# Moving the start addresses of hh, hl, xc0 and set 1's first W1 tile within SBUF to 160 and 96 modulo 256 bytes

## The chip, the cores and the metric

The kernel runs on one core of a Trainium2 chip. The metric is the time of one execution on the device in microseconds (us); the median of several executions is compared. Engines are named as in the profile: PE is TensorE's matmuls and PEld its weight loads, DVE is VectorE, ACT ScalarE, POOL GpSimd, SP SyncE, which here issues DMAs.

## What is computed

A linear-attention scan over 768 steps for 4 batches and 8 heads, a gated two-matrix layer, and then a layer of eight experts whose gate is balanced by eight Sinkhorn rounds. There are 3072 tokens of 384 numbers, 8 experts and 1024 hidden numbers in each. The change touches the experts alone, the last loop below.

```python
def _moe2_ref(x, w_gate, w1, w2) -> np.ndarray:
    N, D = x.shape
    E = w_gate.shape[1]
    logits = x @ w_gate
    ...
    out = np.zeros((N, D), dtype=np.float32)
    for e in range(E):
        h = np.maximum(x @ w1[e], 0.0)
        ye = h @ w2[e]
        out += P[:, e:e + 1] * ye
    return out.astype(np.float32)
```

## The kernel before

All large products are made of numbers in two parts, high and low, each kept as float32r: a product is three matmuls, high by high, high by low, low by high.

The expert stage runs over `n` = 0 to 63, here called phases: 16 pairs of hidden blocks (`k`), and for each the four batches of tokens (`sb`). A phase computes the hidden block of its tokens by a fast matrix product that needs 15 products in place of 18 (the list `ORDER`). Each of the 15 products is six matmuls into `zp` with 256 columns: the moving operand is a token factor `xc`, the stationary one (the weights) a W1 factor `w1c` (`z_prod`, line 881). The factors lie in four groups of 4, 4, 4 and 3 products: tiles `xc0` to `xc3`, and for W1 `w1c{set}{group}` in three sets that take turns. Phase `n` uses two sets: 0 and 1 for k = 0, 3, 6 ..., then 2 and 0, then 1 and 2, so each pair holds for four phases.

VectorE and ScalarE add the products up in `ct`; `h_hi` (line 894) writes the rectified result's high part `hh` on ScalarE and `h_lo` the low part `hl` on VectorE. Both tiles have 8 buffers of 2 x 256 float32.

The second product uses the hidden block as weights: `y_fill` (line 1051) queues 24 units for the tokens of the phase before; a unit is three matmuls into `yp` with 384 columns, `hh` by `w2h`, `hh` by `w2l`, `hl` by `w2h`, where `hh` and `hl` are stationary and `w2h`, `w2l` moving. After each of the 15 products `phase` (line 935) issues as many units as a table written out by hand says:

```python
    YN = dict(zip(ORDER, (3, 2, 0, 3, 3, 0, 1, 1, 1, 1, 2, 2, 2, 1, 99)))
```

So TensorE's row in a phase is six zp, nine yp, six zp, six yp, twelve zp, nine yp, and so on: 90 zp and 72 yp, with 13 stretches of yp between stretches of zp. Where the text speaks of a switch, it means one such change from zp to yp and back. In the first two phases there are fewer yp. After the last phase the remaining yp come in one run.

All matmuls go through one helper, line 114 of the kernel. Tiles are laid out one behind the other in pools; `spaced` (line 623) puts an unused tile ahead of a tag's first tile (or behind it), by the table `GAPS` (line 621) in words of four bytes, which shifts all that follows in that pool. A tag's buffers are used in turn, so a tile's address repeats.

The start addresses in SBUF that follow from it, modulo 256 bytes (further offsets within the tiles are multiples of 512 bytes for W1 factors, hh and hl, 1024 for token factors and 1536 for w2h and w2l):

| operand of the expert stage | role | before | after |
|---|---|---|---|
| `xc0` (group 0) | moving, zp | 224 | 96 |
| `xc1`, `xc2`, `xc3` | moving, zp | 96 | 96 |
| `w1c10` (set 1, group 0) | stationary, zp | 32 | 160 |
| the other eleven `w1c` | stationary, zp | 160 | 160 |
| `hh`, `hl`, 8 buffers each | stationary, yp | 32 | 160 |
| `w2h`, `w2l`, 4 buffers each | moving, yp | 96 | 96 |

In the stage before, pa and pb (128 x 384, moving `xhl`, weights `w1h`, `w1l`, `w2h`, `w2l` of that layer) have both operands at 96.

Of the kernel before, what the change touches and what calls it, by code (L numbers as in the profile page):

```python
# [12 lines left out]
F32R = mybir.dt.float32r  # L13
# [48 lines left out]
def tile_rwkv_moe_sinkhorn_moe(  # L62
# [21 lines left out]
    P = 128  # L84
# [13 lines left out]
    T = 256  # L98
# [77 lines left out]
    pools = {}  # L176
# [415 lines left out]
    XP_ = plan(XC, XB)  # L592
# [25 lines left out]
        return sums, high, low  # L618

    w1raw, w2raw, w1c, w2c, xc, xd = {}, {}, {}, {}, {}, {}  # L620
    GAPS = {'w2h2': 16, 'w2l3+': 16, 'w1c00': 16, 'xc0': 16, 'w1c10': 16, 'xc1': 16, 'w1c01': 16, 'w1c13+': 16}

    def spaced(pool, shape, dtype, tag, name):
        n_ = GAPS.pop(tag, 0)
        if n_:
            pool.tile([P, n_], F32, name="gap_" + tag)
        t = pool.tile(shape, dtype, tag=tag, name=name)
        n_ = GAPS.pop(tag + "+", 0)
        if n_:
            pool.tile([P, n_], F32, name="gap_after_" + tag)  # L630
        return t
# [16 lines left out]
    def sp_w1(i, g, eng, tmp_=None):  # L648
        if i >= NW:
            return ()  # L650
        n_ = len(WP_[g][4])
        k = i % 3
        if tmp_ is None:
            tmp_ = pools["m2"].tile([P, 4, P], F32, tag="w1s", bufs=2, name="w1s")
        t = spaced(pools["m2" if k == 2 else "w"], [P, 2, n_, P], F32R, f"w1c{k}{g}", f"w1c{k}{g}")
        w1c[i, g] = t
        sums, high, low = factors(WP_, g, WB, w1raw[i], tmp_, t, eng)

        def end():
            low()  # L660
            if g == NGR - 1:
                w1raw.pop(i)
                ld_w1(i + 2)

        return sums, high, end

    def sp_w2(i):
        if i >= NW:
            return
        t = w2raw.pop(i)  # L670
        k = i % 4
        pool = pools["m" if k < 2 else "m2"]
        hi = spaced(pool, [P, 2, DM], F32R, f"w2h{k}", f"w2h{k}")
        lo = spaced(pool, [P, 2, DM], F32R, f"w2l{k}", f"w2l{k}")
        nc.scalar.activation(hi, t, AF.Copy)
        nc.vector.tensor_tensor(lo, t, hi.bitcast(F32), op=ALU.subtract)
        w2c[i] = (hi, lo)
        ld_w2(i + 2)

    def x_tile(n, g):  # L680
        t = pools["w" if g < 2 else "m"].tile([P, 2, len(XP_[g][4]), T], F32R, tag=f"xc{g}", name=f"xc{g}")
        xc[n, g] = t
        return t

# [35 lines left out]
    def ld_x(n, g):  # L720
        if n >= NB2 * NS:
            return
        t = x_tile(n, g)
        nc.sync.dma_start(t.bitcast(F32), xd[n % NS, g])
# [167 lines left out]
        return pools["m"].tile([P, 2, T], F32, tag="ct", bufs=CT, name="ct")  # L892

    def h_hi(n, i, b_, src):
        hh = pools["m2"].tile([P, 2, T], F32R, tag="hh", bufs=HB, name="hh")
        hl = pools["m2"].tile([P, 2, T], F32R, tag="hl", bufs=HB, name="hl")
        hb[n, i, b_] = (hh, hl, src)
        nc.scalar.activation(hh, src, AF.Relu)  # L898

# [35 lines left out]
    def phase(n):  # L935
# [71 lines left out]
        def s15():  # L1007
            prod("f", 15, True, True)
            sub(ct["10"], ct["10"], bk["f"])
            h_hi(n, 1, 0, ct["10"])  # L1010
            add(ct["12"], ct["12"], bk["f"])

        def s12():
            prod("h", 12, True, True)
            add(ct["00"], ct["00"], bk["h"])
            h_hi(n, 0, 0, ct["00"])
            h_lo(n, 1, 0)

        def s7():
            prod("e", 7, False, True)  # L1020
            add(ct["8"], ct["8"], bk["e"])
            h_hi(n, 1, 1, ct["8"])
            h_lo(n, 0, 0)
# [72 lines left out]
    CT, HB = 8, 8  # L1096
# [154 lines left out]
```

## Time and profile before

| | |
|---|---|
| median of 3 runs | 1935.41 us (1935.39 to 1937.25) |
| the profiled execution's own time | 1937.41 us |
| its span, first to last instruction | 1935.7 us |
| PE busy | 1908.3 us, 99% |
| DVE busy | 1384.3 us, 72% |
| ACT, POOL busy | 685.5 us, 646.8 us |
| expert stage | from 441.8 us on |

The page lists busy time by engine, the chain of work that ended last, and the groups of like instructions. Matmuls are pipelined: the next begins while the last still drains, so the duration of one (279 ns for a zp matmul) is longer than the distance to the next. Distances are read from the timeline, whose rows give the start of each stretch of like matmuls in us with two decimals.

### The profile page before, as it was taken

How to read it: one execution, taken by the hardware profiler on the slowest of the kernel's cores; microseconds unless marked ns; L12 is line 12 of the kernel's file. 1: busy time of each engine (PE TensorE's matmuls, PEld its weight loads, DVE VectorE, ACT ScalarE, POOL GpSimd, SP SyncE). 2: the span in 40 equal slices, each digit the busy share in tenths (PEclk: the TensorE clock that was granted, in tenths of full speed). 3: DMA queues.
4: the chain of work that ended last, by engine and by line, in shares of the span. 5: the costliest groups of instructions: out<-in, count | busy, mean ns of one | idle time of the engine just before them, and what ended most of it. 6: DMA issues, size and time to landing. Idle time of an engine off the chain costs nothing.

```text
span 1935.7 us, 38115 instructions
## 1 busy us (share of the span) xinstructions
PE 1908.3 (99%) x15499; PEld 1860.5 (96%) x15499; DVE 1384.3 (72%) x2409; ACT 685.5 (35%) x1322; POOL 646.8 (33%) x867
## 2 busy tenths in 40 slices
PE   6999999999999999999999999999999999999999
PEld 3799999999999999999999999999999999999999
DVE  7865787765887886676767676667677767667666
ACT  6733333344333333333333333333333333333322
POOL 6756666635331313122222222222323231312200
PEclk9999999999999999999999999999999999999999
DMA  9622444346655555555555555556455555555453
GB/s 371 231 93 83 139 133 138 104 148 238 234 178 191 191 191 192 180 200 182 197 189 190 187 194 187 189 174 207 172 196 185 193 192 190 189 180 187 171 201 120
DMA packets 90495, 353.76 MB, mean 183 GB/s; under 512 B 10385, under 2 KB 34257, under 8 KB 64593
## 3 DMA queue, kind: packets, MB, share of 16 engines
q1 hardware_dynamic: 90320, 351.34, 52.5%
q8 instruction: 122, 2.00, 0.4%
q14 instruction: 53, 0.43, 0.1%
HBM read 329.67 MB, written 20.45 MB: 181 GB/s over the span
## 4 chain that ended last, share of the span: by engine, by line
PE 95%; DVE 2%; DMA 1%; ACT 1%; SPq 0%; issue 0%; DVEq 0%; ACTq 0%
PE yp L114 41%; PE zp L114 34%; PE po L114 5%; PE pa L114 5%; PE pb L114 5%; PE w34ps L114 1%; PE yt L114 1%; PE sc L114 1%; PE trn L114 1%; DMA nat_kn<-in_kn_dram 1%; PE up L114 1%; DMA raw<-in_moe_w_dram 0%; PE pl L114 0%; DVE cvp L229 0%; DVE Sn L384 0%
## 5 line engine op out<-in xcount | busy, mean ns | idle before, releaser
L114 PE MATMUL zp<-xc,w1c 128*128 128x256 f32 x5760 | 805.3, 279 | 1.1 <-DVE ct L906 0.6
L114 PEld LDWEIGHTS zp<-xc,w1c 128*128 128x128 f32 x5760 | 780.3, 188 | 4.2 <-DVE ct L909 1.4
L114 PE MATMUL yp<-w2h,hl 128*128 128x384 f32 x1536 | 518.5, 338 | 0.6 <-DVE hl L903 0.6
L114 PE MATMUL yp<-w2l,hh 128*128 128x384 f32 x1536 | 517.3, 337 | 0.0
L114 PE MATMUL yp<-w2h,hh 128*128 128x384 f32 x1536 | 514.9, 335 | 0.0
L898 ACT ACTIVATE hh<-ct 128x512 fp32r<-128x512 f32 x384 | 236.8, 632 | 532.8 <-DVE ct L906 268.6
L906 DVE TENSOR_TENSOR ct<-ct,zp 128x512 f32<-128x512 f32 x576 | 380.0, 683 | 50.9 <-PE zp L114 45.8
L616 POOL TENSOR_TENSOR w1c<-w1s,w1c 128x512 fp32r<-128x512 f32 (+1 forms) x120 | 126.8, 1057 | 790.1 <-PE yp L114 484.0
L913 ACT ACTIVATE ct<-zp 128x512 f32<-128x512 f32 x256 | 153.5, 600 | 451.1 <-PE zp L114 451.1
L114 PEld LDWEIGHTS yp<-w2h,hl 128*128 128x128 f32 x1536 | 288.6, 188 | 1.0 <-DVE hl L903 0.9
L114 PEld LDWEIGHTS yp<-w2h,hh 128*128 128x128 f32 x1536 | 288.6, 188 | 0.2 <-issue 0.2
L114 PEld LDWEIGHTS yp<-w2l,hh 128*128 128x128 f32 x1536 | 288.6, 188 | 0.0
L1078 DVE SCALAR_TENSOR_TENSOR acc<-yp,Pm,acc 128x384 f32<-128x384 f32 x336 | 205.6, 612 | 108.2 <-PE yp L114 108.1
L903 DVE SCALAR_TENSOR_TENSOR hl<-ct,hh 128x512 fp32r<-128x512 f32 x384 | 274.8, 729 | 0.0
L909 DVE TENSOR_TENSOR ct<-ct,zp 128x512 f32<-128x512 f32 x128 | 88.0, 687 | 165.2 <-PE zp L114 165.2
L909 DVE TENSOR_TENSOR ct<-zp,ct 128x512 f32<-128x512 f32 x128 | 88.3, 690 | 76.0 <-ACT ct L913 40.7
L616 POOL TENSOR_TENSOR w1c<-w1raw,w1c 128x128 fp32r<-128x128 f32 (+1 forms) x90 | 55.9, 621 | 202.4 <-ACT w1c L612 202.4
L608 POOL TENSOR_TENSOR w1s<-w1raw 128x128 f32<-128x128 f32 x240 | 120.7, 524 | 0.2
L483 POOL TENSOR_TENSOR gl<-gs,gh 128x384 fp32r<-128x384 f32 x64 | 72.9, 1139 | 109.9 <-ACT gh L479 106.8
L114 PE MATMUL pa<-xhl,w1h 128*128 128x384 f32 x384 | 101.7, 345 | 1.3 <-ACT w34s L255 1.3
L114 PE MATMUL pb<-xhl,w2h 128*128 128x384 f32 x384 | 98.1, 336 | 0.4 <-DVE cv L230 0.4
L474 DVE TENSOR_TENSOR gs<-pb,asb 128x384 f32<-128x384 f32 x64 | 35.4, 552 | 68.3 <-PE pb L114 49.5
(130 smaller groups left out, 1908.9 us busy)
## 6 DMA issues: line engine op xcount, KB each, us to landing
xc<-xd SPq DMA_DIRECT2D x192, 1024.0 KB, 4.9
xc<-xd SPq DMA_DIRECT2D x64, 768.0 KB, 4.3
xd<-x2s SPq DMA_DIRECT2D x53, 256.0 KB, 2.7
w1raw<-in_e_w_dram SPq DMA_DIRECT2D x32, 384.0 KB, 3.1
w2raw<-in_e_w_dram SPq DMA_DIRECT2D x32, 384.0 KB, 3.1
raw<-in_moe_w_dram SPq DMA_DIRECT2D x8, 1024.0 KB, 9.3
nat_w<-in_w_dram SPq DMA_DIRECT2D x24, 264.5 KB, 3.6
nat_k<-in_kt_dram SPq DMA_DIRECT2D x24, 256.0 KB, 4.4
```

What stands on the lines that cost most here:

```text
L114: nc.tensor.matmul(o, lhsT, rhs, start=start, stop=stop, **kw)
L474: nc.vector.tensor_tensor(t, m_t.pop(("pb", blk, f)), m_t.pop(("asb", blk, f)), op=ALU.mult)
L483: nc.gpsimd.tensor_tensor(gl[:, f, :], m_t.pop(("gs", blk, f)), gh[:, f, :].bitcast(F32), op=ALU.subtract)
L608: eng.tensor_tensor(tmp_[:, many.index(r), :], at_(a), at_(b), op=ALU.add if sg == 1 else ALU.subtract)
L616: eng.tensor_tensor(lo[:, d0:d1, :], sv, hi[:, d0:d1, :].bitcast(F32), op=ALU.subtract)
L898: nc.scalar.activation(hh, src, AF.Relu)
L903: nc.vector.scalar_tensor_tensor(hl, src, 0.0, hh.bitcast(F32), op0=ALU.max, op1=ALU.subtract)
L906: nc.vector.tensor_tensor(o, a, b_, op=ALU.add)
L909: nc.vector.tensor_tensor(o, a, b_, op=ALU.subtract)
L913: nc.scalar.activation(t, src, AF.Copy)
L1078: nc.vector.scalar_tensor_tensor(dst, yp, so["Pm"][:, tt, e:e + 1], dst, op0=ALU.mult, op1=ALU.add)
```

## The change

Five entries of the gap table: 32 words (128 bytes) ahead of `hh`, 32 behind `hl`, and 48 in place of 16 ahead of `xc0` and `xc1`. For the first two `h_hi` takes its tiles through `spaced`, for the others `x_tile` does; `spaced` passes the number of buffers on. Where the kernel asks for a tile first is where the gap is put, so group 0's `xc0` and set 1's `w1c10`, which lies between `xc0` and `xc1`, move too, and `xc1` and all behind it stay. No instruction is added or taken away, and on every engine the instructions and the semaphores that they wait for stand in the same order in both programs; only numbers in buffer names differ.

```diff
-    GAPS = {'w2h2': 16, 'w2l3+': 16, 'w1c00': 16, 'xc0': 16, 'w1c10': 16, 'xc1': 16, 'w1c01': 16, 'w1c13+': 16}
-
-    def spaced(pool, shape, dtype, tag, name):
+    GAPS = {'hh': 32, 'hl+': 32, 'w2h2': 16, 'w2l3+': 16, 'w1c00': 16, 'xc0': 48, 'w1c10': 16, 'xc1': 48, 'w1c01': 16, 'w1c13+': 16}
+
+    def spaced(pool, shape, dtype, tag, name, **kw):
         n_ = GAPS.pop(tag, 0)
         if n_:
             pool.tile([P, n_], F32, name="gap_" + tag)
-        t = pool.tile(shape, dtype, tag=tag, name=name)
+        t = pool.tile(shape, dtype, tag=tag, name=name, **kw)
...
     def x_tile(n, g):
-        t = pools["w" if g < 2 else "m"].tile([P, 2, len(XP_[g][4]), T], F32R, tag=f"xc{g}", name=f"xc{g}")
+        t = spaced(pools["w" if g < 2 else "m"], [P, 2, len(XP_[g][4]), T], F32R, f"xc{g}", f"xc{g}")
...
     def h_hi(n, i, b_, src):
-        hh = pools["m2"].tile([P, 2, T], F32R, tag="hh", bufs=HB, name="hh")
-        hl = pools["m2"].tile([P, 2, T], F32R, tag="hl", bufs=HB, name="hl")
+        hh = spaced(pools["m2"], [P, 2, T], F32R, "hh", "hh", bufs=HB)
+        hl = spaced(pools["m2"], [P, 2, T], F32R, "hl", "hl", bufs=HB)
```

## Rows read from the trace of the kernel before

**Rows 1.** The page's first part: busy us, share of the span, instructions.

```profile
PE 1908.3 (99%) x15499; PEld 1860.5 (96%) x15499; DVE 1384.3 (72%) x2409; ACT 685.5 (35%) x1322; POOL 646.8 (33%) x867
```

**Rows 2.** The page's chain that ended last: share by engine, then by line.

```profile
PE 95%; DVE 2%; DMA 1%; ACT 1%; SPq 0%; issue 0%; DVEq 0%; ACTq 0%
PE yp L114 41%; PE zp L114 34%; PE po L114 5%; PE pa L114 5%; PE pb L114 5%; PE w34ps L114 1%; PE yt L114 1%; PE sc L114 1%; PE trn L114 1%; DMA nat_kn<-in_kn_dram 1%; PE up L114 1%; DMA raw<-in_moe_w_dram 0%; PE pl L114 0%; DVE cvp L229 0%; DVE Sn L384 0%
```

**Rows 3.** Groups of instructions: busy us, mean ns of one, idle before.

```profile
L114 PE MATMUL zp<-xc,w1c 128*128 128x256 f32 x5760 | 805.3, 279 | 1.1 <-DVE ct L906 0.6
...
L114 PE MATMUL yp<-w2h,hh 128*128 128x384 f32 x1536 | 514.9, 335 | 0.0
```

**Rows 4.** Windows, the expert stage: PE, PEld, DVE, ACT, POOL busy, clock, DMA, GB/s.

```profile
441.80:1932.00 1490.20, 1488.52 (x10479) 1484.38 (x10478) 1059.90 (x1731) 488.40 (x908) 374.86 (x601) 1.00 0.55 190
```

**Rows 5.** Timeline of PE, groups 1 to 3 of one phase: start, length, instructions.

```profile
1168.36 0.86 PE L114 MATMUL zp<-xc,w1c 128*128 128x256 f32 x6
1169.05 0.33 PE L114 MATMUL yp<-w2h,hh 128*128 128x384 f32 x1
...
1170.62 1.54 PE L114 MATMUL zp<-xc,w1c 128*128 128x256 f32 x12
1171.99 0.33 PE L114 MATMUL yp<-w2h,hh 128*128 128x384 f32 x1
...
1172.52 0.86 PE L114 MATMUL zp<-xc,w1c 128*128 128x256 f32 x6
1173.21 0.33 PE L114 MATMUL yp<-w2h,hh 128*128 128x384 f32 x1
...
1176.18 0.86 PE L114 MATMUL zp<-xc,w1c 128*128 128x256 f32 x6
...
1184.35 0.51 PE L114 MATMUL zp<-xc,w1c 128*128 128x256 f32 x3
```

**Rows 6.** Timeline of PE, run of yp at the end: first and 72nd.

```profile
1919.54 0.34 PE L114 MATMUL yp<-w2h,hh 128*128 128x384 f32 x1
...
1931.84 0.34 PE L114 MATMUL yp<-w2h,hl 128*128 128x384 f32 x1
```

**Rows 7.** Timeline of PE, run of pa and pb: first row and 33rd matmul.

```profile
387.87 0.51 PE L114 MATMUL pa<-xhl,w1h 128*128 128x384 f32 x2
...
393.41 0.34 PE L114 MATMUL pb<-xhl,w2l 128*128 128x384 f32 x1
```

**Rows 8.** Timeline of PE, group 0 of the phase of rows 5.

```profile
1161.36 0.87 PE L114 MATMUL zp<-xc,w1c 128*128 128x256 f32 x6
...
1163.62 0.86 PE L114 MATMUL zp<-xc,w1c 128*128 128x256 f32 x6
1164.33 0.34 PE L114 MATMUL yp<-w2h,hh 128*128 128x384 f32 x1
...
1165.36 1.58 PE L114 MATMUL zp<-xc,w1c 128*128 128x256 f32 x12
1166.78 0.34 PE L114 MATMUL yp<-w2h,hh 128*128 128x384 f32 x1
```

**Rows 9.** Timeline of PE, first zp of phases 8, 12, 16 and 20.

```profile
632.90 0.28 PE L114 MATMUL zp<-xc,w1c 128*128 128x256 f32 x1
...
724.74 0.28 PE L114 MATMUL zp<-xc,w1c 128*128 128x256 f32 x1
...
816.64 0.28 PE L114 MATMUL zp<-xc,w1c 128*128 128x256 f32 x1
...
908.63 0.40 PE L114 MATMUL zp<-xc,w1c 128*128 128x256 f32 x2
```

## The prediction

> **What bounds the kernel now.** I read the busy shares first: TensorE works 99% of the span, VectorE, the next, 72% [rows 1]. The chain that ended last says the same: 95% of it is PE, and zp and yp alone are 75% [rows 2]. Both are made in the last stage, the experts, from 441.8 us to 1932 us; there PE is busy 1488.5 of 1490.2 us, and the granted clock is 1.00 throughout, its upper level of 2.4 GHz [rows 4]. So no engine releases time there; what counts is how far apart matmuls start. The mean durations of the groups (279 and 335 ns) are no guide to that, since matmuls overlap [rows 3]. I therefore took differences of start stamps in the timeline, over many matmuls because a stamp has 10 ns.
>
> Three numbers come out. A **zp** matmul (256 columns) that follows zp matmuls of its kind: the run of 12 takes 1171.99 - 1170.62 = 1.37 us up to the next yp, a run of 6 takes 1169.05 - 1168.36 = 0.69; the six more cost 0.68, or 113.3 ns each [rows 5]. A **yp** matmul (384 columns) among yp matmuls: 71 steps in 1931.84 - 1919.54 = 12.30 us, 173.2 ns each [rows 6]. A **switch**: three rounds of six zp and three yp take 1176.18 - 1172.52 = 3.66 us, 1.220 each, where 6 x 113.3 + 3 x 173.3 = 1.200 would do [rows 5]. So each change from zp to yp and back costs 20 ns. The rest of that phase says it again: from its second group to the next phase are 66 zp, 48 yp and 10 switches, 1184.35 - 1168.36 = 15.99 us against 7.48 + 8.32 = 15.80, or 19 ns a switch [rows 5].
>
> **Does the address matter at all?** One place in this trace compares addresses with nothing else changed. In group 0 the moving tile xc0 begins at 224 modulo 256 and the weights at 160 (set 0 or 2) or 32 (set 1); in groups 1 to 3 it is always 96 and 160. The phase that begins at 1161.36 uses sets 2 and 0, so 224 against 160. Its run of 12 zp takes 1166.78 - 1165.36 = 1.42 us, 0.05 more than the run at 96 against 160: some 4 ns a matmul [rows 5, 8]. The whole group takes 1168.36 - 1161.36 = 7.00 us for 24 zp, 24 yp and three switches, where 2.72 + 4.16 = 6.88 is the sum without switches: 40 ns a switch in place of 20 [rows 5, 8]. And the phases differ by set pair, four at a time: 91.84 us with sets 1 and 2, 91.90 with 0 and 1, 91.99 with 2 and 0 [rows 9]. Same instructions, same counts: only addresses differ. The Trainium skill (TensorE: Matmul & The Clock Gate, Part 2, step 1) holds that PE has two independent read ports, so that loading the next weights doesn't steal bandwidth from the running matmul. By that rule addresses would be worth nothing and the time would stay; the 1.42 against 1.37 us speaks against it here.
>
> **The change, part by part.** No instruction is added, removed or moved; each engine's order and its waits stay as they are. Only start addresses change: xc0 from 224 to 96, set 1's group 0 of W1 from 32 to 160, all eight hh and eight hl from 32 to 160. The gap tiles cost no instruction. Neighbours (w2h and w2l at 96, w1s and w1c at 160) keep their place modulo 256. ACT writes hh and DVE writes hl as before; VectorE has 28% spare [rows 1].
>
> Part 1, **xc0 and set 1**. All zp then stand at 96 against 160, so group 0 should cost what groups 1 to 3 cost. A phase would take 90 x 113.3 + 72 x 173.3 = 22.68 us plus 13 switches of 20 ns, 22.94; four take 91.76. Against the three set pairs that saves 0.08, 0.14 and 0.23 us, together 0.45 in twelve phases [rows 9]. Sixty-four phases give **-2.4 us**. This part has one answer: the value is read from the same products at the new addresses.
>
> Part 2, **hh and hl**. They are the weights of all 4608 yp matmuls, and the trace holds no yp with weights at 160. Two prices have to be bounded.
>
> First the steady yp. Weights at 32 give 173.2 ns [rows 6]. The stage before has matmuls of 384 columns too, pa and pb, with both operands at 96: 32 steps in 393.41 - 387.87 = 5.54 us, 173.1 ns each [rows 7]. Two distances between the operands (64 and 0), one time. I take the same for the third and put it at 0. The bounds: below, 384/256 x 113.3 = 170 ns, the rate zp has at 96 against 160, so -3.2 ns; above, what the bad pair costs a zp, +4 ns [rows 8].
>
> Second the switch. Now the weights jump from 160 to 32 and back at each switch, besides the width going from 256 to 384; after the change only the width changes. Rows that switch without a jump do not exist. A run without a switch costs nothing extra (113.3 and 173.2 ns), a switch with the jump 20 ns, and one where the moving tile jumps as well 40 ns [rows 5, 8]. That the price doubled when a second address jumped is what makes me think that jumps carry much of it; that the width too has a share I can't exclude. Bounds 0 and 20 ns; it is as near to the one row as to the other, and I take 10. There are 13 switches in each of 62 phases, with the first two phases some 820. Half of 820 x 20 ns = 16.4 us is **-8.2 us**, with 0 and -16.4 as ends.
>
> The sum: -2.4 - 8.2 = -10.6 us. The profiled execution took 1937.4 us by its own time, 1.7 around a span of 1935.7; the median of the three runs shown is 1935.41. The profiled one becomes 1926.8, the median **1924.8 us**. PE stays the bound: DVE's 1060 us in the stage [rows 4] are far from 1480.
>
> **The rivals.**
>
> *yp gets slower.* The switch into zp loads weights at 160 during a yp matmul, and the loss shows just there and in the zp behind it. If weights at 160 disturb the moving rows at 96 in a 384-column matmul, then after the change not 820 but all 4608 yp pay. Price: up to the 4 ns that a zp pays for its bad pair [rows 8], 18.4 us; less the 2.4 of part 1, 1951 us. It decides from 0.5 ns a yp (2.4 us / 4608). Half of it, with the switches unchanged, gives 1942. For it: the one stage in which 160 meets 384 columns is the switch, and it costs. Against: zp at this very pair runs at the floor of the rows, and two other distances leave yp at 173.
>
> *hh and hl do nothing.* Steady yp at 173.2 for any address, and the 20 ns belong to the change of width. Then only part 1 remains: 1933.0, within what a measurement can tell from no change. For it: pa and pb equal yp. The skill's rule above would go further and give 1935.4; both count as no change, and I give the two together one chance.
>
> *yp gets faster too.* If yp at 96 against 160 falls to 170 ns as zp's rate suggests, 3.2 ns x some 3800 yp that follow a yp is 12 us more: with part 1 and half of the switches 1912.6, with all of the switches 1904. For it: 113.3 is 256 columns plus 6.25%, 173.2 is 384 plus 8.3%. Against: pa and pb, at another distance, show no such floor.
>
> *The change doesn't do what it says*: a gap goes into a pool once, at a tag's first tile, and all later tiles of a tag reuse its places, so all eight buffers of hh move. I give it no chance of its own.
>
> **How the numbers follow.** Forecast (part 1 and a part of the switches) 0.42; yp faster too 0.10; nothing from hh and hl 0.20; yp slower 0.28. A measurement of this kernel tells about 0.2% (3.9 us) from no change. Faster by more than that: the forecast and the faster rival, 0.52 together, less 0.02 for a forecast whose switches save next to nothing, 0.50. Within: 0.20 and those 0.02, and 0.02 of the slower rival near its deciding point: 0.24. Slower: 0.26. The forecast's own range goes from 1916.6 (all of the switches) to 1931.5. Eight in ten: from 1913, half of the faster rival, to 1944, which takes in the slower rival up to half of its price and a little more.
>
> **What would show it.** Part 1: four phases take the same whatever the set pair, and a run of 12 zp in group 0 takes 1.37 us. The switch: a round of six zp and three yp below 1.22 us; at 1.20 all of it is gone. The steady yp: 71 steps at the end in 12.30 us if I am right, 12.07 if the fast rival is, 12.6 or more if yp got slower. Wrong altogether would be a yp above 173.5 ns, since 4608 of them outweigh every switch. What I can't see in this trace is any yp with weights at 160, and the sign hangs on it.

## The result and the profile after

The changed kernel takes **1919.12 us** (median of 5, 1917.88 to 1919.88) against 1935.41 before: 16.3 us less by the medians. The ratio over all runs of the two is 0.9911, with a 95% interval of 0.9901 to 0.9921. Its profiled execution took 1919.88 us around a span of 1918.2, 17.5 us less than the one of before. One execution of e7 below (3149.55 us, at a granted clock of 0.56) is left out; the others whose clock is on record ran at 1.00.

The page of the changed kernel, busy time by engine, the chain's shares by engine, and the zp group (busy us, mean ns of one):

```profile
PE 1891.9 (99%) x15499; PEld 1843.2 (96%) x15499; DVE 1377.1 (72%) x2409; ACT 685.0 (36%) x1322; POOL 648.2 (34%) x867
...
PE 94%; DVE 2%; DMA 2%; ACT 1%; issue 0%; SPq 0%; DVEq 0%; ACTq 0%
...
L114 PE MATMUL zp<-xc,w1c 128*128 128x256 f32 x5760 | 793.0, 277 | 0.9 <-DVE ct L906 0.6
```

Nothing else has become the bound [rows 1, 2]. PE has the same 15499 instructions and is busy 16.4 us less. The mean duration of a zp falls only from 279 to 277 ns [rows 3], so the page alone doesn't tell where the time went. The window of the expert stage does: same start, the same 10479 matmuls, same clock, and PE busy 1471.05 us for 1488.52, 17.5 us less [rows 4].

```profile
441.80:1914.40 1472.60, 1471.05 (x10479) 1466.58 (x10477) 1055.88 (x1731) 487.60 (x908) 375.98 (x601) 1.00 0.55 192
```

Timeline of PE in the changed kernel (start, length, instructions), group 0 of the same phase as in [rows 5, 8]:

```profile
1153.16 0.85 PE L114 MATMUL zp<-xc,w1c 128*128 128x256 f32 x6
...
1157.13 1.53 PE L114 MATMUL zp<-xc,w1c 128*128 128x256 f32 x12
1158.50 0.33 PE L114 MATMUL yp<-w2h,hh 128*128 128x384 f32 x1
```

The same phase from group 1 on; the last row is the next phase's first zp:

```profile
1160.05 0.85 PE L114 MATMUL zp<-xc,w1c 128*128 128x256 f32 x6
...
1162.29 1.53 PE L114 MATMUL zp<-xc,w1c 128*128 128x256 f32 x12
1163.66 0.33 PE L114 MATMUL yp<-w2h,hh 128*128 128x384 f32 x1
1164.17 0.85 PE L114 MATMUL zp<-xc,w1c 128*128 128x256 f32 x6
...
1167.77 0.85 PE L114 MATMUL zp<-xc,w1c 128*128 128x256 f32 x6
...
1175.85 0.62 PE L114 MATMUL zp<-xc,w1c 128*128 128x256 f32 x4
```

The run of 12 zp takes 1.37 us in group 0 as in group 1 (1.42 and 1.37 before). Three rounds of six zp and three yp take 1167.77 - 1164.17 = 3.60 us, 1.200 each where it was 1.220: the **switch costs nothing** any more. From group 1 to the next phase it is 1175.85 - 1160.05 = 15.80 us, the sum of 66 zp and 48 yp without any switch; group 0 takes 6.89 us for a sum of 6.88 (7.00 before).

The last run of yp, first row and 71 steps later, against [rows 6]:

```profile
1902.04 0.34 PE L114 MATMUL yp<-w2h,hh 128*128 128x384 f32 x1
...
1914.35 0.34 PE L114 MATMUL yp<-w2h,hl 128*128 128x384 f32 x1
```

12.31 us: the steady yp has not moved. First zp of phases 8, 12, 16 and 20, against [rows 9]:

```profile
631.21 0.51 PE L114 MATMUL zp<-xc,w1c 128*128 128x256 f32 x3
...
721.99 0.51 PE L114 MATMUL zp<-xc,w1c 128*128 128x256 f32 x3
...
812.76 0.51 PE L114 MATMUL zp<-xc,w1c 128*128 128x256 f32 x3
...
903.53 0.51 PE L114 MATMUL zp<-xc,w1c 128*128 128x256 f32 x3
```

Four phases take 90.78, 90.77, 90.77 us whatever the set pair, 22.69 each, against 22.96 to 23.00 before. A step is the time from the start of one matmul to the start of the next. Summed over the stage from the trace's start stamps, what the steps take above 113.3 ns a zp and 173.3 a yp has gone from 19.1 us to 1.7, while the longer gaps and the stage's few other matmuls (most of both in the first phases) stay at 19.5 us.

### The profile page after: what moved, and what is told of

It is laid out like the page before. It is cut to its first block, busy times and chain, and to the rows that moved or that the text cites. A ratio compares the mean times of both kernels' runs of the same rounds, so it can differ in the third digit from the quotient of the medians.

```text
span 1918.2 us, 38115 instructions
## 1 busy us (share of the span) xinstructions
PE 1891.9 (99%) x15499; PEld 1843.2 (96%) x15499; DVE 1377.1 (72%) x2409; ACT 685.0 (36%) x1322; POOL 648.2 (34%) x867
## 4 chain that ended last, share of the span: by engine, by line
PE 94%; DVE 2%; DMA 2%; ACT 1%; issue 0%; SPq 0%; DVEq 0%; ACTq 0%
PE yp L114 41%; PE zp L114 34%; PE po L114 5%; PE pa L114 5%; PE pb L114 5%; PE yt L114 1%; DMA raw<-in_moe_w_dram 1%; PE w34ps L114 1%; PE sc L114 1%; PE trn L114 1%; DMA nat_kn<-in_kn_dram 1%; PE up L114 0%; PE pl L114 0%; DVE cvp L229 0%; DVE Sn L384 0%
## 5 line engine op out<-in xcount | busy, mean ns | idle before, releaser
L114 PE MATMUL zp<-xc,w1c 128*128 128x256 f32 x5760 | 793.0, 277 | 0.9 <-DVE ct L906 0.6
L114 PEld LDWEIGHTS zp<-xc,w1c 128*128 128x128 f32 x5760 | 766.5, 188 | 4.4 <-DVE ct L909 1.0
```

What stands on the lines that cost most here:

```text
L114: nc.tensor.matmul(o, lhsT, rhs, start=start, stop=stop, **kw)
```

## The experiments

The gap table is written here by what it gives: the start, modulo 256 bytes, of the moving operands (xc, w2h, w2l) and of the weights (w1c, hh, hl). "Distance" is the first less the second; it is 192 in the changed kernel (96 - 160), and 64 where before has hh and hl at 32. The texts on record call J the theory that the price lies in the jump of an address at a switch, P that each pair of addresses has a price of its own for every step, Q that a yp could fall to 170 ns. They call a zp a first-layer step and a yp a second-layer step. The kernel before took 1936.7 to 1936.8 us beside these runs.

**One part at a time.** The first kernel has part 1 alone, the second part 2 alone.

```diff
 e1_zp_alone
-    GAPS = {'hh': 32, 'hl+': 32, 'w2h2': 16, ..., 'xc0': 48, 'w1c10': 16, 'xc1': 48, ...}
+    GAPS = {'w2h2': 16, ..., 'xc0': 48, 'w1c10': 16, 'xc1': 48, ...}
 e2_yp_alone
+    GAPS = {'hh': 32, 'hl+': 32, 'w2h2': 16, ..., 'xc0': 16, 'w1c10': 16, 'xc1': 16, ...}
```

> Part 1 alone: xc0 at 96 and set 1's group 0 at 160, hh and hl stay at 32. Two theories are to be told apart in these runs. Theory J (jump): a switch costs because start addresses modulo 256 change between matmuls that follow each other; with no jump it is free whatever the address. Theory P (pair): what counts is that weights at 160 and moving rows at 96 fit together; any other pair costs. For this run both say what the prediction's first part says: group 0 falls to the price of groups 1 to 3, 20 ns a switch, a phase takes 22.94 us whatever the set pair, and the time falls by 2.4 us to 1933.0 (median).

> Part 2 alone: hh and hl at 160, xc0 stays at 224 and set 1's group 0 at 32. If the two parts add up, the time is the changed kernel's plus part 1: 1919.1 + 2.4 = 1921.5 us. In groups 1 to 3 the switches cost nothing, in group 0 still 20 to 40 ns each. J and P agree here; if the parts don't add up (say a gain under 10 us), each part needs the other, which neither says.

e1: 1932.62 us (10 runs), ratio 0.9979 (0.9969 to 0.9988), -4.2 us. e2: 1929.54 us (4 runs), 0.9961 (0.9947 to 0.9976), -7.3 us. Together -11.5, where both at once gave -16.3: **the parts don't add up.** The traces say so too: part 1 takes a mean phase from 22.98 us to 22.92 when hh and hl stand at 32, and from 22.86 (e2) to 22.69 when they stand at 160. Timeline of PE in e1: the run of 12 in group 0, and three rounds:

```profile
1162.45 1.52 PE L114 MATMUL zp<-xc,w1c 128*128 128x256 f32 x12
1163.81 0.33 PE L114 MATMUL yp<-w2h,hh 128*128 128x384 f32 x1
...
1169.53 0.86 PE L114 MATMUL zp<-xc,w1c 128*128 128x256 f32 x6
...
1173.19 0.86 PE L114 MATMUL zp<-xc,w1c 128*128 128x256 f32 x6
```

Group 0 is healed (1.36 us), and the round still takes 1.220. In e2 the rounds are free, and group 0 is not; a phase with sets 2 and 0:

```profile
1161.36 1.58 PE L114 MATMUL zp<-xc,w1c 128*128 128x256 f32 x12
1162.78 0.34 PE L114 MATMUL yp<-w2h,hh 128*128 128x384 f32 x1
...
1166.63 1.58 PE L114 MATMUL zp<-xc,w1c 128*128 128x256 f32 x12
1168.04 0.34 PE L114 MATMUL yp<-w2h,hh 128*128 128x384 f32 x1
...
1169.78 0.85 PE L114 MATMUL zp<-xc,w1c 128*128 128x256 f32 x6
...
1170.98 0.85 PE L114 MATMUL zp<-xc,w1c 128*128 128x256 f32 x6
```

The second of these runs of 12 stands in group 1, at 96 against 160 as in the changed kernel, and takes 1.41 us, not 1.37. In the next phase of e2, with sets 1 and 2, where half of group 0's zp are at distance 192 (224 - 32), the same run of group 1 is back at 1.36:

```profile
1189.52 1.53 PE L114 MATMUL zp<-xc,w1c 128*128 128x256 f32 x12
1190.88 0.33 PE L114 MATMUL yp<-w2h,hh 128*128 128x384 f32 x1
```

So a run's time is not set by its own addresses alone: what went before it has a part. That it was the other pair in group 0 that spoiled group 1 is not shown, since e9 below has the same 1.41 there with all starts at 96 and 160.

**Other distances, no jumps.** All moving operands at one start and all weights at another, so that no address jumps modulo 256 at a switch. Where room was short, the tiles mask and eye moved from the kernel's constants to the scan stage's pool (e3, e5 to e9).

```diff
 e3_96_32: moving 96, weights 32     e4_96_96: 96, 96     e5_224_32: 224, 32
 e6_96_224: 96, 224     e10_96_128: 96, 128     e11_96_192: 96, 192
-    GAPS = {'hh': 32, 'hl+': 32, 'w2h2': 16, 'w2l3+': 16, 'w1c00': 16, 'xc0': 48, ...}
+    GAPS = {'w2h2': 16, 'w2l3+': 48, 'w1c00': 48, 'xc0': 16, ...}   (e3; the others likewise)
```

> All weights at 32 (hh, hl as in the kernel before, all twelve W1 tiles moved from 160 to 32) and all moving tiles at 96: one pair throughout, as in the changed kernel, but another pair. To make room, two small constants of the scan stage (mask and eye) lie in that stage's own pool. J: no address jumps, switches are free, 1919 us. P: zp now has the distance (64) that cost 4 ns a matmul in group 0 before: 5760 x 4 = 23 us above the changed kernel, 1942 us, and slower than before.

> All weights and all moving tiles at 96, one pair throughout with distance 0. J: no jump, 1919 us. P: another pair than 160 and 96, so zp above 113.3 ns each; no row has a zp at this distance, and from the 4 ns of distance 64 an estimate is 0 to 4 ns, 1919 to 1942 us. Steady yp 173.3 ns by both, as pa and pb at this pair.

> All moving tiles at 224 and all weights at 32: both moved by 128 against the changed kernel, so their distance modulo 256 is the same, 192. (mask and eye lie in the scan stage's pool for room.) Theory P, sharpened after the first runs: each distance between moving and stationary start has its own steady price for a zp (113.3 ns at 192, some 118 at 64 and more at 0), a yp takes 173.3 ns at any. If the distance is what counts: 1919 us as the changed kernel. If the addresses 96 and 160 themselves count: zp at 118 or more, 1943 us or above.

> Moving tiles at 96, all weights at 224: distance 128, the one of the four that no run has had. Theory P gives zp a price of its own between those seen, 113.3 to 119 ns: 1919 to 1949 us; yp at 173.3. If only distance 192 is free, above 1935; if the price falls with the distance (0: 119, 64: 118, 192: 113.3), some 115.5 ns and 1932 us.

> All moving operands at 96 and all stationary ones at 128, distance 224. Theory S (each distance of the moving start from the weights' start has its own price for a step, and 192 is one of several free ones): 1919 us, if 224 is free. Theory T (192 alone is free; 64, 0 and 128 cost 4.5 to 5.9 ns on each of 4900 first-layer steps in runs, and 224 lies between 192 and 0): 1930 to 1950 us, first-layer steps 115 to 118 ns. A second-layer step below 173.3 ns in either case would be the first time that it moves, and would show a pair better than the changed kernel's: 3.3 ns x 4608 = 15 us, 1904 us.

> All moving operands at 96 and all stationary ones at 192, distance 160. Theory S (several distances are free, and 160 is one): 1919 us. Theory T (192 alone is free, and 160 lies between 192 and 128, the dearest one): 1930 to 1955 us, first-layer steps 115 to 119 ns. A second-layer step below 173.3 ns would give 1904 us.

Medians, and from the timelines the run of 12 zp in group 1, 71 yp of the last run, and a steady phase:

| distance | kernel | us | ratio to before (95%) | 12 zp | 71 yp | phase |
|---|---|---|---|---|---|---|
| 192 | changed | 1919.1 | 0.9911 (0.9901 to 0.9921) | 1.36 | 12.31 | 22.69 |
| 192 | e5 (224, 32) | 1919.8 | 0.992 (0.9897 to 0.9942) | 1.41* | 12.31 | 22.86* |
| 64 | e3 | 1943.6 | 1.0033 (1.0022 to 1.0045) | 1.41 | 12.31 | 23.09 |
| 160 | e11 | 1948.9 | 1.0062 (1.0047 to 1.0077) | 1.42 | 12.31 | 23.17 |
| 0 | e4 | 1949.5 | 1.0065 (1.0049 to 1.0082) | 1.43 | 12.31 | 23.20 |
| 224 | e10 | 1950.0 | 1.0069 (1.0054 to 1.0084) | 1.42 | 12.31 | 23.21 |
| 128 | e6 | 1958.9 | 1.0112 (1.0095 to 1.0129) | 1.43 | 12.50 | 23.35 |

*) the profiled run of e5 alone took 1928.26 us; its three others 1918.14 to 1920.02. More on it below. The changed kernel's 1.36 is 1.363 by the trace's own stamps; the rows above, whose stamps have 10 ns, give 1.37.

TensorE's same instructions in the same order take anything from 1919 to 1959 us. Two expectations were missed: P had 1942 us as its upper end for e4 and 1949 for e6, and both came out above. e3 decides between J and P: it has no jumps at all, hh and hl where before has them, and is 24.5 us slower than the changed kernel, and 14.9 slower than e9 below, which has mask and eye in the same place as e3. Timeline of e3: the run of 12 in group 1, and one round:

```profile
1174.30 1.58 PE L114 MATMUL zp<-xc,w1c 128*128 128x256 f32 x12
1175.71 0.34 PE L114 MATMUL yp<-w2h,hh 128*128 128x384 f32 x1
...
1177.45 0.87 PE L114 MATMUL zp<-xc,w1c 128*128 128x256 f32 x6
...
1178.68 0.87 PE L114 MATMUL zp<-xc,w1c 128*128 128x256 f32 x6
```

Every zp now takes 1.41 / 12, nearly 118 ns, and the round 1.23. J falls: the switch is free in e3, as J said (6 x 1.41/12 + 3 x 0.1733 = 1.225), but every step pays. e5 keeps the distance and moves both starts by 128: 1919.8, so at this one other place the distance counts and not the place. Of the six distances tried, 192 alone lets a zp run at 113.3 ns, which is theory T of e10 and e11 (e10 came in at the very top of its range); S, by which several would, falls. Distances 32 and 96 were not tried. A yp in a long run takes the same 173.4 ns at five of them; only at 128 does it pay too, in the last run of e6:

```profile
1941.36 0.34 PE L114 MATMUL yp<-w2h,hh 128*128 128x384 f32 x1
...
1953.86 0.34 PE L114 MATMUL yp<-w2h,hl 128*128 128x384 f32 x1
```

12.50 us for 71 steps, 176.1 ns each.

**Longer stretches, and Q.** e8 lets the table issue yp in even numbers of units, which makes fewer switches; e7 does this and places w2l at 224 for the even hidden blocks and w2h at 224 for the odd ones, so that moving starts alternate from yp to yp. Both have mask and eye moved.

```diff
 e8_even, e7_alt
-    YN = dict(zip(ORDER, (3, 2, 0, 3, 3, 0, 1, 1, 1, 1, 2, 2, 2, 1, 99)))
+    YN = dict(zip(ORDER, (4, 2, 0, 2, 4, 0, 2, 0, 2, 0, 2, 2, 2, 0, 99)))
 e7_alt
+    GAPS: 'w2l0': 32, 'w2l1': 32, 'w2l2': 32, 'w2l3': 32
```

> The changed kernel's addresses, with the table of yp units per product made even (4, 2, 0, 2, 4, 0, 2, 0, 2, 0, 2, 2, 2, 0 and the rest): 10 switches a phase in place of 13. It is also the control for e7_alt. In the changed kernel a switch costs nothing, so nothing changes: 1919 us. If a switch still had a price of 5 ns, 3 x 5 ns x 62 = 1 us less.

> As e8_even, with the moving tiles of the yp alternating between 96 and 224: w2h 96 and w2l 224 for the even hidden block, w2h 224 and w2l 96 for the odd one, so that in a run of yp every start is 128 bytes from the one before. In the changed kernel the first yp behind a zp takes 170 ns to the next start and the following ones 173.3. Theory Q: the row reads of a 384-column matmul end half a turn of 256 bytes off, so the next one fits at once if it begins 128 bytes further; then all 4608 yp take 170: 3.3 ns x some 3800 yp is 12.5 us less than e8_even, 1906 us. Rival: a yp takes 173.3 wherever it begins, or each jump costs: not below e8_even, up to 4 ns x 4608 = 18 us above it.

e8: 1928.55 us (4 runs), 0.9956 (0.9942 to 0.9971), and 1919 was expected. e7: 1934.5 us (9 runs), 0.9989 (0.998 to 0.9999), 6.0 us above e8. In e7 the 71 yp of the last run take 12.46 us, 2 ns each more than at one start; behind the first of them none takes less than 172 ns, so Q falls. (Its premise was off too: 384 numbers of four bytes are six turns of 256 bytes, with no half turn left.) e8's miss can be read in its trace; here group 0's run of 12, group 1's first six zp, and group 1's run of 12:

```profile
1161.59 1.53 PE L114 MATMUL zp<-xc,w1c 128*128 128x256 f32 x12
1162.96 0.33 PE L114 MATMUL yp<-w2h,hh 128*128 128x384 f32 x1
...
1164.00 0.95 PE L114 MATMUL zp<-xc,w1c 128*128 128x256 f32 x6
1164.78 0.34 PE L114 MATMUL yp<-w2h,hh 128*128 128x384 f32 x1
...
1166.88 1.58 PE L114 MATMUL zp<-xc,w1c 128*128 128x256 f32 x12
1168.29 0.34 PE L114 MATMUL yp<-w2h,hh 128*128 128x384 f32 x1
```

Group 0's run of 12 takes 1.37 us as in the changed kernel. The six zp behind it take 0.78 in place of 0.69: only six yp stand ahead of them where the old table has nine, and the first one's weight load waits for VectorE, which still reads the bank of zp that they add to (its instruction of line 909 ends at 1163.92, the load starts at 1163.97). Behind this wait the run of 12 takes 1.41. Against the changed kernel's trace that makes 5.4 us more of gaps (24.9 for 19.5) and 4.0 us more in the steps (5.7 for 1.7), together e8's miss of 9.4 us. So the new table brings a wait into each phase, and the steps behind it run slower.

**The control, and a second course.** e9 is the changed kernel with mask and eye moved, nothing else. It was meant to show that this costs nothing.

```diff
 e9_room
-    mask = const.tile([P, DP], F32, name="mask")
-    eye = const.tile([P, DP], F32, name="eye")
...
+    mask = att.tile([P, DP], F32, name="mask")
+    eye = att.tile([P, DP], F32, name="eye")
```

> The changed kernel with mask and eye in the scan stage's pool and nothing else altered: the ground on which e3 to e8 stand, whose addresses or tables needed that room. If the place of these two tiles is nothing to the routed-expert loop, as all theories take it: 1919 us, phases of 22.69 us, a first-layer step 113.3 ns in a run. If e8's 1928.5 us or e3's 1943.6 us came in part from the room and not from the tables or the addresses, this kernel stands above 1921 us by that part.

It takes 1928.76 us (5 runs, 1927.31 to 1929.39), 0.9956 (0.9942 to 0.997): 9.6 us above the changed kernel, with every operand at the same start modulo 256. (hh, hl, set 2 of W1 and half of the w2 tiles lie 512 bytes lower, the others where they were.) The time is e8's to within 0.2 us, but the trace is another. Timeline of PE in e9, the phase that answers to the one shown above: runs of 12 in groups 0 and 1:

```profile
1161.13 1.58 PE L114 MATMUL zp<-xc,w1c 128*128 128x256 f32 x12
1162.54 0.34 PE L114 MATMUL yp<-w2h,hh 128*128 128x384 f32 x1
...
1166.40 1.58 PE L114 MATMUL zp<-xc,w1c 128*128 128x256 f32 x12
1167.81 0.34 PE L114 MATMUL yp<-w2h,hh 128*128 128x384 f32 x1
```

The first two runs of six zp in this phase go at 113.3 ns, the run of 12 behind them at 1.41 / 12, and so does group 1 into its last six zp; from group 2 on the rounds take 1.20 again. Every phase from number 7 on repeats this: 22.86 us against 22.69, and 57 phases of 0.167 us are 9.5 of the 9.6 us. The profiled run of e5 shows the same 22.86 while its three other runs took the changed kernel's time. So, by these times, **one program at distance 192 has two courses that keep themselves**: in one the stream is thrown out once a phase, at group 0's run of 12, and stays at 118 ns a zp for thirty of them; in the other it comes back within three zp.

What comes at that place can be read in both traces. It is the one spot in a phase where a weight load starts late. First the changed kernel, then e9, with the weight loads (PEld) and ScalarE (ACT); the last row of each is the load for the run of 12:

```profile
1156.34 0.60 ACT L913 ACTIVATE ct<-zp 128x512 f32<-128x512 f32 x1 [1.70 <-PE zp L114]
...
1156.77 0.34 PE L114 MATMUL yp<-w2l,hh 128*128 128x384 f32 x1
1156.78 0.19 PEld L114 LDWEIGHTS yp<-w2h,hl 128*128 128x128 f32 x1
...
1156.95 0.34 PE L114 MATMUL yp<-w2h,hl 128*128 128x384 f32 x1
1156.99 0.45 PEld L114 LDWEIGHTS zp<-xc,w1c 128*128 128x128 f32 x3
```

```profile
1160.35 0.60 ACT L913 ACTIVATE ct<-zp 128x512 f32<-128x512 f32 x1 [1.70 <-PE zp L114]
...
1160.96 0.34 PE L114 MATMUL yp<-w2h,hl 128*128 128x384 f32 x1
1161.00 0.44 PEld L114 LDWEIGHTS zp<-xc,w1c 128*128 128x128 f32 x3
```

ScalarE copies the bank of zp that the run's first product adds to, and the load waits for that copy: it starts 0.05 us after the copy's end and 0.04 us after the start of the matmul ahead of it, where other loads start within 0.01 us. Every kernel of this document has this late load, 30 to 50 ns in nearly all phases and 40 in the kernel before, so the change didn't bring it. In the changed kernel the load is 46 ns late, the run starts 8 ns late (the yp ahead takes 181 ns in place of 173), and the next two zp take 6 and 3 ns more. In e9 the load is 44 ns late, the run starts on time, and all its zp take 118. Whether those few ns choose the course is not shown, nor why e9 always took the dearer one (5 runs) and the changed kernel never (5 runs). That distances modulo more than 256 bytes have a part in e9 is not excluded, though e5 took either time at one set of addresses.

**One weight in three displaced.**

```diff
 e12_hh160_hl32
-    GAPS = {'hh': 32, 'hl+': 32, ...}
+    GAPS = {'hh': 32, 'hl': 32, ...}
```

> The changed kernel with the low halves of the activations (hl, the weights of one second-layer product in three) back at 32, and all else as changed. If a stretch in another pair throws the stream out, and it needs some five first-layer steps to come back, then one second-layer step in three at distance 64 suffices for the price wherever hl stands last before the first-layer steps: with e1's 1932.6 us for both halves at 32 as the upper end and 1919 us as the lower one, 1924 to 1933 us, the switches that follow an hl product at 20 to 40 ns and the others at 0. If the price goes by the share of displaced steps instead, a third of e1's 13.5 us: 1923.6 us, spread evenly over all switches. If the second-layer steps alone matter and not the last one, 1919 us.

1929.26 us (4 runs), 0.9963 (0.9948 to 0.9978): in the range of the first theory and above the second one's 1923.6. The pattern is neither's. (The phase takes 22.86 us as in e9, but its excess lies in the rounds.) Timeline of PE: three rounds with three yp, then one with six yp:

```profile
1167.97 0.86 PE L114 MATMUL zp<-xc,w1c 128*128 128x256 f32 x6
...
1171.63 0.86 PE L114 MATMUL zp<-xc,w1c 128*128 128x256 f32 x6
...
1173.37 0.85 PE L114 MATMUL zp<-xc,w1c 128*128 128x256 f32 x6
...
1175.09 0.85 PE L114 MATMUL zp<-xc,w1c 128*128 128x256 f32 x6
```

3.66 us for three rounds is 20 ns a switch, while 1175.09 - 1173.37 = 1.72 us is 0.68 + 1.04, nothing extra; yet both end with an hl at 32. After three or nine yp the switch costs 20 ns, after six none. So the last pair alone doesn't decide, nor the share of displaced ones; the length of the stretch has a part. Why is not shown.

## Why the prediction was right, point by point

The forecast was 1924.8 us, faster, with an own range from 1916.6 to 1931.5; the time is 1919.1.

*The bound, the zp and yp in runs.* As foretold: PE at 99% before and after, 113.3 ns a zp, and the steady yp at 12.31 us for 71 steps (12.30 foretold, 12.07 if faster, 12.6 if slower). The step "Two distances between the operands (64 and 0), one time. I take the same for the third" held, and held for 160 and 224 too, but not in general: at 128 a yp takes 176.1 ns.

*Part 1, -2.4 us.* Alone it gave -4.2 (interval -2.3 to -6.0), with phases of 22.92 us for 22.94 foretold, whatever the set pair. Right in place; in size the forecast lies at the edge of what was measured.

*Part 2, -8.2 us: the term that was mis-sized.* Of the 20 ns a switch the prediction said "it is as near to the one row as to the other, and I take 10". Measured: the round went to 1.200, all 20 ns. On top of part 1 that is worth 1932.6 - 1919.1 = 13.5 us, between the 8.2 taken and the 16.4 of the far end; in e1 not all 13 switches cost 20 ns any more (the one into group 0's run of 12 cost nothing, 1.36 us above). The far end needs the change of width to cost nothing, and at one distance throughout it does cost nothing.

*The reason behind it was wrong.* "That the price doubled when a second address jumped" misread [rows 8]: of the 0.12 us that group 0 takes above its sum, the 24 zp at the prediction's own 4 ns each are 0.10, so it is the steps that pay there and not the switches. And the run of 12 in those rows is no place "with nothing else changed": it is the one behind the late weight load, and e9 has 1.41 us there at 96 against 160. That distance 64 costs over 4 ns a zp came out right all the same, by e3. There no address jumps, and every zp pays.

What [rows 5] showed as the price of a switch is a slow start of the zp behind a stretch of yp at distance 64. By the trace's start stamps the first five take 117, 117, 119, 116 and 114 ns, 16 of the 20 ns above 113.3 each; in the changed kernel only the first two take more, 116 and 114, and the first yp, at 170, gives it back. So the parts were not to be summed one by one: with two thirds of group 0 still off 192, part 2 gave -7.3; with both, -16.3, of which e9's course would keep -7.9. The forecast lies between the times of the two courses, 1919 and 1929, which e5 took with one and the same program. No row of before could tell which one the loop would take; that it took the cheaper one is luck as far as the prediction goes.

*The rivals.* yp slower by its pair: not at 192, though e6 shows that the mechanism exists (128). hh and hl do nothing: e2's -7.3 us, with an interval that leaves out 1, rules it out. The Trainium skill (TensorE: Matmul & The Clock Gate, Part 2, step 1) gives TensorE two independent read ports; read as the prediction did, that addresses would change nothing, it doesn't agree with these runs, 1919 to 1959 us by start addresses alone. yp faster too: no, 71 steps took 12.31 us, and e7 made them no faster.

## What to carry to other kernels

Where matmuls run back to back with new weights each, read the distance between like starts from the timeline run by run. A few ns that differ between groups with equal instructions may come from addresses; look first whether a weight load there starts late, since here that alone went with the same few ns (e8, e9). Try the distance between moving and stationary starts as a setting of its own, for all pairs at once: one part alone can show less than its share. And give every variant that moves tiles its control, since a move that keeps every start modulo 256 cost more than half of such a gain here. Two variants with the same time need not lose it in the same place (e8, e9, e12): compare their traces.

## What the hardware showed that was not expected

- These hold for float32r with new weights for each matmul, at a granted clock of 1.00. In a run of 12, a zp of 256 columns starts 113.3 ns after the last at distance 192 (modulo 256 bytes) and some 118 to 119 ns at 0, 64, 128, 160 and 224; in a long run, a yp of 384 columns takes 173.4 ns at all but 128, where it takes 176.1.
- At distance 192 the stream can run at either pace: 113.3 or, behind a weight load 44 ns late, 118 ns for some 30 zp, with the yp between them (e9, group 0's run of 12 and most of group 1). The two courses of a loop differ by 0.17 us in 22.7.
- A weight load that waits for another engine started 0.05 us after that engine's instruction ended (ScalarE in the changed kernel and e9, VectorE in e8). The profile's list of waits shows none of it where the matmuls ahead keep TensorE busy.
- Whether a displaced product costs anything at the next switch depends on how many yp the stretch has: 20 ns after 3 or 9, none after 6 (e12).
